# Splitting the first two input loads by head parity, and five idle matmuls in front of the last expert's rows, in a one-core attention and mixture kernel

## The chip, the cores and the metric

The kernel runs on one core of a Trainium2 chip. The core has five engines that work side by side: TensorE (PE, matrix products, with its weight loads listed apart as PEld), VectorE (DVE), ScalarE (ACT), GpSimd (POOL) and SyncE (SP), which here only issues transfers. Sixteen DMA engines move data between the chip's main memory and the core's memory. The metric is the device time of one execution in microseconds (us); lower is better.

## The reference

```python
def _attn_ref(r, k, v, w, u):                       # r, k, v: (4, 8, 768, 48), w, u: (8, 48)
    state = np.zeros((B, H, D, D))
    for t in range(S):
        kt, vt, rt = (k[:, :, t], v[:, :, t], r[:, :, t])
        cur = np.einsum('bhd,bhe->bhde', u[None] * kt, vt)
        y[:, :, t] = np.einsum('bhd,bhde->bhe', rt, state + cur)
        state = w[None, :, :, None] * state + np.einsum('bhd,bhe->bhde', kt, vt)

def _moe_ref(x, phi, w1, w2):                       # x: (3072, 384), phi: (384, 32), w1: (8, 384, 1024), w2: (8, 1024, 384)
    logits = x @ phi
    d = softmax(logits, axis=0)                     # over the tokens
    slot_input = (d.T @ x).reshape(E, 4, D)
    for e in range(E):
        slot_out[e] = np.maximum(slot_input[e] @ w1[e], 0.0) @ w2[e]
    c = softmax(logits, axis=1)                     # over the slots
    return c @ slot_out
```

A linear attention with a decaying state runs over four batches of 768 steps with eight heads of width 48. Its output, seen as 3072 tokens of width 384, goes through a soft mixture: each of eight experts has four slots, a slot is a weighted mean of all tokens, each expert runs two matrix products on its slots, and each token takes a weighted mean of the 32 results.

## The kernel before, in words

The kernel is a list of small named tasks. The string `ORDER` at the top (lines 9 to 31) gives the order in which they are emitted, and with it the order of the instructions on every engine; nothing is reordered later. An engine runs its own instructions strictly in that order and waits where one needs another engine's or a transfer's result.

**Front.** The inputs come in eight pieces m = 0 to 7, two for each batch: an even piece has 256 time steps of all eight heads, an odd one 512. Tasks `Lk`, `Lr` and `Lv` load k, r and v of a piece; all are issued by SP with `load_f` (line 192). In the tile, partition p holds eight (odd pieces: sixteen) consecutive steps of one head pair, first the even head, then the odd head. The source view puts the time blocks first, then the eight heads. A whole k or r of an even piece is one transfer of 256 runs of 1536 bytes, 384 KB. The decay vector w is loaded by ACT at line 211, and u by SP (task `LU`, line 381), between `Lr0` and `Lv0`.

`Sk0` and `Sr0` multiply the first k and r by tables of decay powers (line 427, on DVE for piece 0, mostly on POOL afterwards). The tables come from w: a logarithm on ACT (line 283), products on DVE (line 281), exponentials on ACT (line 287 and line 288). Then PE transposes the pieces (line 436), forms the attention scores (line 506) and the states, and writes the tokens' rows.

**Weights.** The 16 expert matrices are loaded by POOL with a conversion to bf16 (tasks `W0` to `W15`, lines 783 and 785) as buffers come free. The last one, the second matrix of the eighth expert, is in two transfers: `W15a` has seven of its eight row blocks and `W15` the last.

**Tail.** `Q00` to `Q13` (line 921) multiply the hidden values by the experts' second matrices and sum into one accumulator. `Q11` has the third expert of the second group, `Q12` the last expert's first seven row blocks (waits for `W15a`), and `Q13` its eighth (waits for `W15`). ACT copies the sum (`so`, line 928). Then 24 output rows of 128 tokens each are formed by PE (line 949), copied alternately by ACT and DVE (lines 951 and 953) and written by SP in eight transfers of 1, 2, 3, 4, 4, 4, 4 and 2 rows (line 955). Row 0 is made in two halves, one for each copying engine.

**Idle products.** A word such as `F19a_4` in `ORDER` stands for matmuls whose results nobody reads (line 861): the number after the underscore is the amount in units of 256 columns, issued as matmuls of up to 512 columns; the letter a says that they write the score accumulator `Ab`.

**Transfers and their semaphores.** The trace's instructions show that the transfers of SP and ACT take eight semaphores in turn, and that a transfer waits until the one eight places earlier has landed.

Of the kernel before, what the change touches and what calls it, by code (L numbers as in the profile page):

```python
# [26 lines left out]
NB1 L3 AL2 ET2 YE11 AC1 ZT2 RM3 EE2 ZC3 EX3 SU2 F10a_3 X111 X110 XE111:ACT AL3 F11a_1 ET3 W15a ND1 XE110 EE3:ACT LB4  # L27
RM4 DP2 G1 DP3 AC2 EX4 G2 ET4 AL4 G3 G5 LC2 GS EE4 F12_3 DP4 AC3 ZT3 AC4 LX1 NM2 NB2 F13a_1 MG UN SU3 LC3 F14_6 H00
R00:DVE NM3 H01 R01 F15a_5 HT00 ND2 W15 HT01 HE00 F16a_1 Q00 HE01 Q01 H11 LE1:ACT R11 H10 LX2 R10:DVE NB3 LT4 ND3:ACT
SU4 F18a_2 HT11 HT10 HE10 HE11:ACT LC4 NM4 NB4 ND4:DVE Q10 LE2 LX3 LX4 LE3 F19a_4 Q11 Q12 LE4:ACT Q13  # L30
"""


# [12 lines left out]
class _Plan:  # L46
# [7 lines left out]
    def buf(self, pool):  # L54
        return _Buf(pool)

    def add(self, name, engs, fn, deps=(), bufs=()):
        self.by[name] = _Task(name, engs, fn, list(deps), list(bufs))
# [23 lines left out]
def kernel(  # L82
# [13 lines left out]
    B, H, S, D = r.shape  # L96
# [11 lines left out]
    R = 8  # L108
# [5 lines left out]
    CC = NS // U3  # L114
# [11 lines left out]
    def O(ins):  # L126
        return tc.keep_in_program_order(ins)

    pe, dve, act, pool, sp = nc.tensor, nc.vector, nc.scalar, nc.gpsimd, nc.sync
# [5 lines left out]
    RW = 2 * J * D  # L135
# [53 lines left out]

    def load_f(dst, a, m):
        b, lg = divmod(m, 2)
        jn = J if lg else JH
        O(sp.dma_start(out=dst[:, 0:2 * jn * D].rearrange("p (e x) -> p e x", e=2),  # L195
                       in_=a[b].rearrange("h (y j) d -> y h (j d)", j=jn)[lg * CC * R:lg * CC * R + 32]))

# [146 lines left out]
    def consts_d():  # L344
# [5 lines left out]
    L = _Plan(dict(raw=raw, ks=ks_t, vj=vj_t, kn=kn_t, vn=vn_t, AT=AT_t, prs=pr_t[0:1], prl=pr_t[1:2], dv=dv_t,  # L350
                   **{f"{x}T": t for x, t in turned.items()},
                   S=S_t, Z=Z_t, x=x_t, zc=zc_t, Lc=Lc_t, Lcl=[Lc_t[0][:, NS - 2:]], Lsl=[Ls_t[0][:, NS - 2:]], Ls=Ls_t, E=E_t, ET=ET_t, T=T_t, A=[Ab], Y=[Yb], M=[Mb], **{f"xT{j}": [t] for j, t in enumerate(xT_t)}))
    buf, add = L.buf, L.add
# [17 lines left out]
    for m in range(NLD):  # L371
        for i, nm in enumerate("krv"):

            b, o = (kr["k", m][0], RH) if nm == "r" and m % 2 == 0 else (buf("raw"), 0)
            kr[nm, m] = b, o
            add(f"L{nm}{m}", "SP", (lambda b, o, a, m: lambda t: load_f(b.inst[:, o:RW], a, m))(b, o, (k, r, v)[i], m), bufs=[b])

    def load_phi(t):
        O(sp.dma_start(out=phi_f, in_=moe_phi.rearrange("(p q) s -> p q s", q=nM)))
# [13 lines left out]
    for h, av_, x in (("a", argl, slice(0, JH + 1)), ("b", argm, slice(JH, J + 1))):  # L393
        add(f"AH{h}", "DVE", (lambda av_, x: lambda t: argv_part(av_, e17l[:, x]))(av_, x))
        for i in range(2):

            add(f"TB{i}{h}", "ACT", (lambda i, h, av_: lambda t: O(act.activation(  # L397
                out=tabl[i][:, :, JH:J] if h == "b" else tabl[i][:, :, 0:JH],
                in_=av_[:, :, 1 - i:JH + 1 - i], func=AF.Exp, scale=(-1.0, 1.0)[i])))(i, h, av_),
# [3 lines left out]
    for m in range(NLD):  # L403
        lg = m % 2
        pb = TT["p", m] = buf("pr" + "sl"[lg])
        for nm in "krv":
            dstT = TT[nm, m] = buf(nm + "sl"[lg] + "T")
            P = P2 if nm == "v" else 128
            for h in range(1 + lg):
# [11 lines left out]
                else:  # L421
                    i = "kr".index(nm)
# [42 lines left out]
    for n in range(NU):  # L465
# [4 lines left out]
        m = 2 * bt + (ui > 0)  # L470
# [50 lines left out]
        def f_su(t, Mf=Mf, kn=kn, vn=vn, Sold=Sold, pb=pb, n=n, NK=NK):  # L521
# [13 lines left out]
            bufs=[Mf, vn, pb_, kn] + ([Sold] if ui else []))  # L535
# [26 lines left out]
        def f_y(t, Yf=Yf, rT=rT, vn=vn, dvb=dvb, Sold=Sold, Smid=Smid, a=tuple(ATb), n=n):  # L562
# [18 lines left out]
            bufs=[Yf, rTb, vn, dvb, Smid, ATb[0], ATb[1]] + ([Sold] if ui else []))  # L581
# [213 lines left out]
    for n in range(2 * E):  # L795
        wat[n] = buf("raw")
        wat[n].left += 4
        bufs, deps = [wat[n]], []
# [6 lines left out]
    nm = nm_t[(NPC - 1) % 2]  # L805
# [14 lines left out]
        bufs=[SXb])  # L820
# [118 lines left out]
    i = 0  # L939
# [46 lines left out]
```

## Time and profile before

| | us |
|---|---|
| median of three runs (118.89 to 119.31) | 119.17 |
| the profiled execution's own time | 120.24 |
| its span in the profile | 118.5 |
| PE busy | 98.0 (83%) |
| DVE busy | 94.8 (80%) |
| ACT busy | 86.6 (73%) |
| POOL busy | 61.0 (52%) |
| data moved by the DMA engines | 31.81 MB written to their targets, mean 268 GB/s |

The profile is of one execution, and times below are in microseconds from the start of its span. The span is 1.7 us shorter than that execution's own time, and the profiled execution took 1.1 us more than the median of the runs without a profile. A busy share is an average over stages that differ: what decides is what ended the last wait of each stage.

### The profile page before, as it was taken

To read this page: it belongs to the slowest core of one execution; us is meant where nothing else is said; L and a number is where in the kernel's file an instruction comes from. 1 tells how busy PE (TensorE), PEld (TensorE's weight loads), DVE (VectorE), ACT (ScalarE), POOL (GpSimd) and SP (SyncE) were. 2 spreads that over 40 slices of the span, in tenths; PEclk is the share of its full clock that TensorE was granted. 3 is DMA by queue.
4 is the path that set the end of the run, shared out by engine and by line. 5 is a ranking of instruction groups with operands and counts; after the bars stand their busy time and mean duration, and the time that the engine had idled before them with its cause. 6 is when DMAs were issued, how large, how long until landed. Compare 5 with 4: busy or idle time off the path is not lost.

```text
span 118.5 us, 3926 instructions
## 1 busy us (share of the span) xinstructions
PE 98.0 (83%) x1660; PEld 71.1 (60%) x1660; DVE 94.8 (80%) x180; ACT 86.6 (73%) x140; POOL 61.0 (52%) x79
## 2 busy tenths in 40 slices
PE   3997895999999999989999989999899985498000
PEld 0364674787888787867788878686453542254000
DVE  6899987898999999999999989999786274099100
ACT  5769894999999999989899799979644151269000
POOL 7605899999999989999999010002303000000000
PEclk9999999999999999999999999999999999869955
DMA  2999999999999999999999999999999995059994
GB/s 31 333 387 374 364 408 397 383 390 401 384 384 391 297 229 223 219 215 214 217 212 221 210 223 207 223 207 219 212 212 218 216 207 104 12 199 407 419 402 166
DMA packets 10441, 31.81 MB, mean 268 GB/s; under 512 B 1080, under 2 KB 4408, under 8 KB 10424
## 3 DMA queue, kind: packets, MB, share of 16 engines
q0 software_dynamic: 2448, 12.58, 51.8%
q1 hardware_dynamic: 7832, 18.93, 42.3%
q8 instruction: 13, 0.21, 0.7%
q10 hardware_dynamic: 144, 0.05, 0.2%
q14 instruction: 4, 0.03, 0.1%
HBM read 39.42 MB, written 4.72 MB: 373 GB/s over the span
## 4 chain that ended last, share of the span: by engine, by line
PE 32%; DMA 23%; POOL 15%; DVE 9%; ACT 6%; issue 4%; SPq 3%; DVEq 0%; ACTq 0%; POOLq 0%
DMA raw<-in_moe_w_dram 16%; POOL mix L427 12%; PE T L436 7%; DMA raw<-in_r_dram 7%; PE Ab L506 3%; DVE mix L953 2%; PE Yb L572 2%; SPq L195 2%; PE T L491 2%; PE Yb L567 2%; DVE AT_all L511 2%; ACT xT_all L359 2%; PE Yb L578 2%; PE T L481 2%; PE T L595 2%
## 5 line engine op out<-in xcount | busy, mean ns | idle before, releaser
L427 POOL TENSOR_TENSOR mix<-raw,tabl 128x768 bf16<-128x768 f32 x15 | 27.7, 1858 | 5.8 <-ACT tabl L397 5.4
L511 DVE TENSOR_TENSOR AT_all<-Ab,mask 128x1024 bf16<-128x1024 f32 x24 | 29.3, 1219 | 1.1 <-PE Ab L506 0.5
L359 ACT COPY mix<-T 128x1024 bf16<-128x1024 bf16 x19 | 19.1, 1021 | 3.9 <-PE T L436 2.3
L436 PEld LDWEIGHTS <-mix 128*128 128x128 bf16 x192 | 11.8, 99 | 2.3 <-DVE mix L427 0.7
L555 DVE TENSOR_TENSOR dv<-vn,Mb 128x768 bf16<-128x768 bf16 x12 | 11.4, 946 | 1.4 <-PE Mb L545 1.1
L427 POOL TENSOR_TENSOR mix<-raw,tabs 128x768 bf16<-128x768 f32 x6 | 10.8, 1815 | 0.0
L359 ACT COPY vT_all<-T 96x1024 bf16<-96x1024 bf16 x10 | 10.2, 1021 | 0.5 <-PE T L436 0.4
L506 PE MATMUL Ab<-mix 64*128 64x128 bf16 x192 | 9.5, 218 | 1.2 <-ACT mix L359 1.0
L359 ACT COPY xT_all<-T 128x768 bf16<-128x768 bf16 (+1 forms) x12 | 9.3, 784 | 1.3 <-PE T L595 1.3
L359 ACT CAST x<-Yb 128x768 bf16<-128x768 f32 x12 | 9.7, 808 | 0.0
L436 PE MATMUL T<-turnl,mix 128*128 128x128 bf16 x128 | 9.6, 219 | 0.1
L359 ACT COPY vn<-T 128x768 bf16<-128x768 bf16 x11 | 8.8, 814 | 0.0
L452 DVE TENSOR_TENSOR pr<-T,mix 128x1024 bf16<-128x1024 bf16 x12 | 8.0, 681 | 0.0
L712 POOL TENSOR_TENSOR Lc<-Ls,sm 128x192 bf16<-128x192 f32 x2 | 1.0, 516 | 13.5 <-ACT E L690 13.5
L506 PEld LDWEIGHTS <-mix 64*128 64x128 bf16 x192 | 5.8, 94 | 3.5 <-issue 0.7
L572 PEld LDWEIGHTS <-AT_all 128*128 128x128 bf16 x192 | 6.6, 96 | 1.6
L359 ACT COPY kn<-T 128x768 bf16<-128x768 bf16 (+1 forms) x10 | 7.2, 722 | 0.1
L418 POOL CAST vj<-raw 128x768 bf16<-128x768 f32 x8 | 6.7, 832 | 0.6 <-POOL phi_s L336 0.6
L436 PEld LDWEIGHTS <-vj 128*96 128x96 bf16 x96 | 6.2, 123 | 1.2 <-issue 0.2
L572 PE MATMUL Yb<-vn,AT_all 128*128 128x48 bf16 x192 | 6.8, 183 | 0.0
L539 DVE TENSOR_TENSOR Z<-Mb,wT 128x384 bf16<-128x384 f32 x12 | 6.6, 553 | 0.1
L481 PE MATMUL T<-ident,mix 128*128 128x128 bf16 x80 | 6.1, 219 | 0.2
(187 smaller groups left out, 237.8 us busy)
## 6 DMA issues: line engine op xcount, KB each, us to landing
raw<-in_moe_w_dram POOLq DMA_DIRECT2D x13, 768.0 KB, 14.4
raw<-in_k_dram SPq DMA_DIRECT2D x4, 768.0 KB, 12.2
raw<-in_r_dram SPq DMA_DIRECT2D x4, 768.0 KB, 12.2
raw<-in_v_dram SPq DMA_DIRECT2D x4, 768.0 KB, 12.2
out_dram<-mix SPq DMA_DIRECT2D x3, 768.0 KB, 4.6
raw<-in_k_dram SPq DMA_DIRECT2D x4, 384.0 KB, 10.9
raw<-in_r_dram SPq DMA_DIRECT2D x4, 384.0 KB, 10.6
raw<-in_v_dram SPq DMA_DIRECT2D x4, 384.0 KB, 10.8
```

The lines of the kernel that those rows point to most:

```text
L195: O(sp.dma_start(out=dst[:, 0:2 * jn * D].rearrange("p (e x) -> p e x", e=2), in_=a[b].rearrange("h (y j) d -> y h (j d)", j=jn)[lg * CC * ...
L359: O(act.copy(dst, src))
L418: O(act.copy(o, i_) if t.eng == "ACT" else pool.tensor_copy(o, i_))
L427: O(eng.tensor_mul(src.inst.rearrange("p (j e s) -> p e j s", j=JH, e=2)[:, :, :, 0:D], rv(), tab))
L436: O(pe.transpose(Tb.inst[0:P, jj * 128:(jj + 1) * 128], sv[:, jj, :], (turn, turnl)[lg][:]))
L452: O(dve.tensor_mul(cv(pb), tv(), cv(kT)))
L481: O(pe.transpose(Tb.inst[:, x * 128:(x + 1) * 128], kT.inst[:, x, :], ident[:]))
L506: O(pe.matmul(Abf.inst[:, e, x * C:(x + 1) * C], kT.inst[s, g * nQ + x, :], rT.inst[s, g * nQ + x, :]))
L511: O(dve.tensor_mul(AT.inst[:], Abf.inst[:].rearrange("p e (g t) -> p e g t", g=nQ), mask[:, None, None, :].to_broadcast([128, 2, nQ, C])))
L539: O(dve.tensor_mul(Smid.inst[:], Mf.inst[:, 0:SW].rearrange("p (q d) -> p q d", q=nQ)[:, :, None, :].to_broadcast([128, nQ, 2, D]), wT[:, ...
L555: O(dve.tensor_mul(dvb.inst[:].rearrange("p g e d -> p (g e) d"), vn.inst[:].rearrange("p g e d -> p (g e) d"), Mf.inst[:, 448:448 + 2 * P ...
L572: O(pe.matmul(y[:, x // nQ, q * P2 + e * D:q * P2 + (e + 1) * D], a[x // nQ].inst[:, e, q, :], vn.inst[:, x, e, :], start=False, stop=(c = ...
```

## The change

`load_f` gets a switch. With it, a load becomes two transfers: first the even heads of all time blocks, then the odd heads, each 128 runs of 1536 bytes (192 KB) into its half of every partition's row. The switch is set for the first k and the first r alone (piece 0). Every later load, and the first v, is unchanged. In `ORDER` one word is added, `F20a_10` between `Q11` and `Q12`: five idle matmuls of 512 columns into `Ab`.

```diff
-SU4 F18a_2 HT11 HT10 HE10 HE11:ACT LC4 NM4 NB4 ND4:DVE Q10 LE2 LX3 LX4 LE3 F19a_4 Q11 Q12 LE4:ACT Q13
+SU4 F18a_2 HT11 HT10 HE10 HE11:ACT LC4 NM4 NB4 ND4:DVE Q10 LE2 LX3 LX4 LE3 F19a_4 Q11 F20a_10 Q12 LE4:ACT Q13
...
-    def load_f(dst, a, m):
+    def load_f(dst, a, m, halves=False):
         b, lg = divmod(m, 2)
         jn = J if lg else JH
+        if halves:
+
+            for e in range(2):
+                O(sp.dma_start(out=dst[:, e * jn * D:(e + 1) * jn * D],
+                               in_=a[b].rearrange("(q e) (y j) d -> e y q (j d)", e=2, j=jn)[e, lg * CC * R:lg * CC * R + 32]))
+            return
         O(sp.dma_start(out=dst[:, 0:2 * jn * D].rearrange("p (e x) -> p e x", e=2),
...
-            add(f"L{nm}{m}", "SP", (lambda b, o, a, m: lambda t: load_f(b.inst[:, o:RW], a, m))(b, o, (k, r, v)[i], m), bufs=[b])
+            add(f"L{nm}{m}", "SP", (lambda b, o, a, m, hv: lambda t: load_f(b.inst[:, o:RW], a, m, hv))(b, o, (k, r, v)[i], m, m == 0 and i < 2), bufs=[b])
```

## The prediction

> **What bounds the kernel now.** I read the page's 40 slices first.
>
> ```profile
> PEclk9999999999999999999999999999999999869955
> DMA  2999999999999999999999999999999995059994
> GB/s 31 333 387 374 364 408 397 383 390 401 384 384 391 297 229 223 219 215 214 217 212 221 210 223 207 223 207 219 212 212 218 216 207 104 12 199 407 419 402 166
> ```
>
> The DMA row is the bound: full from the second slice (3 us) to the 33rd (98 us). The GB/s row halves from 40 us on because the weights arrive as half-size bf16; read as fp32 they are about 430 GB/s, the same pace. A stretch in which the DMA engines have nothing to do near the start is not made up later. After the hole at 100 us comes a second full stretch, the output.
>
> The chain of waits shows how the two stretches are joined:
>
> ```profile
> 82.73 18.82 DMA raw<-in_moe_w_dram
> 101.56 0.04 issue
> 101.60 0.51 PE Yb L921 x7
> 102.10 0.01 issue
> 102.11 0.34 PE Yb L921
> ```
>
> W15a is issued at 82.73 and lands at 101.56: 18.8 us for 672 KB, so it stands in a queue. Q12 runs as soon as it lands, Q13 after W15, then `so` at 102.47. So the end is the start of the transfer stream, its bytes, the 2.4 us from W15a to the first output product at 103.00, and the output.
>
> The windows: two of half a microsecond at the start, three of 1 us at the tail, and two of 3.41 us (columns: stretch, its length, busy time and instructions of PE, PEld, DVE, ACT, POOL, granted PE clock, DMA share, GB/s):
>
> ```profile
> 2.50:3.00 0.50, 0.00 (x0) 0.00 (x0) 0.50 (x4) 0.49 (x2) 0.50 (x5) 1.00 0.62 116
> 3.00:3.50 0.50, 0.34 (x3) 0.26 (x4) 0.50 (x4) 0.50 (x4) 0.50 (x4) 1.00 0.89 273
> ```
>
> ```profile
> 99.00:100.00 1.00, 0.42 (x8) 0.13 (x9) 0.00 (x1) 0.00 (x0) 0.00 (x0) 1.00 0.45 82
> 100.00:101.00 1.00, 0.00 (x0) 0.00 (x0) 0.00 (x0) 0.00 (x0) 0.00 (x0) 1.00 0.25 45
> ...
> 103.00:104.00 1.00, 1.00 (x5) 0.69 (x5) 0.45 (x2) 0.32 (x1) 0.00 (x0) 0.50 0.06 16
> ```
>
> ```profile
> 99.19:102.60 3.41, 1.06 (x16) 0.27 (x8) 0.00 (x0) 0.13 (x1) 0.00 (x0) 1.00 0.20 36
> ...
> 17.27:20.68 3.41, 2.13 (x36) 1.67 (x34) 2.43 (x4) 1.93 (x3) 3.41 (x3) 1.00 1.03 399
> ```
>
> The first two lines show the stream of loads starting and not yet full at 3 us. At the tail PE is idle from 99.42 to 101.60. Its granted clock falls to 0.50 at 102.60 and is back at 106.01, one stretch of 3.41 us. The first record of full clock is at 7.03, and 102.60 is 28 times 3.413 us later, so the clock seems to be judged on a grid of 3.41 us by what PE did in the stretch before: PE was busy 1.06 of 3.41 us (31%) ahead of the fall, and the least busy stretch that kept the full clock had 2.13 us (62%).
>
> Last, the timeline of SP's queue:
>
> ```profile
> 0.73 0.71 SPq L195 DMA_DIRECT2D raw<-in_k_dram  x1
> 1.49 0.80 SPq L195 DMA_DIRECT2D raw<-in_r_dram  x1
> 2.35 0.53 SPq L381 DMA_DIRECT2D LexpT<-in_u_dram  x1
> 2.91 0.60 SPq L195 DMA_DIRECT2D raw<-in_v_dram  x1
> ...
> 103.94 1.07 SPq L955 DMA_DIRECT2D out_dram<-vT_all  x2
> 105.83 3.61 SPq L955 DMA_DIRECT2D out_dram<-mix  x4
> ```
>
> By the packet records k's first packet starts at 2.42, 1.69 us after its issue began; r's follow at 4.0 and v's at 4.97 without a hole.
>
> **Part 1, the halves.** Removed: two issues, 0.71 + 0.80 with 0.05 behind each, 1.61 us. Added: four issues of 128 runs. Nearest rows: the first two output transfers, also from SP and also 128 pieces, take 0.35 each; w on ACT, 128 pieces from the same kind of source view, takes 0.63; u, four pieces, 0.53. So a half costs 0.35 to 0.63. I take 0.40: the output rows are the same queue and count, plus a little because k's first issue took 0.71 where v's, the same shape, took 0.60. Four are 4 x (0.40 + 0.05) = 1.80, so u, v0 and all behind them on SP are issued 0.19 later. v0 would start at 3.10, and its packets could flow by 3.10 + 1.69 = 4.79.
>
> The gain: a half has fewer runs to prepare, so its packets may start earlier. From end of issue to first packet k needed 0.98 and the first output 0.85 - 0.35 = 0.50 us (packets from 104.79). With the issue over at 1.13 that is 1.63 to 2.11 against 2.42, a gain of 0.31 to 0.79; w, with as many pieces, had its first packet at 2.16, a gain of 0.26; if the 1.69 runs from the start of the issue whatever the size, nothing. I take 0.31. Then k and r are through by 4.97 - 0.31 = 4.66, and v0's packets at 4.79 leave a hole of 0.13. Net 0.18, say **-0.20**, and since the DMA row never opens, it arrives at W15a whole. Ends: -0.79, and +0.74 (all four at 0.63: v0 issued 1.11 later, at 4.02, its packets at 5.71 against 4.97).
>
> Beside it: Sk0 and Sr0 wait for both halves, but start at 5.46 and about 6.3, when tables and DVE come free; k lands at 4.86 and r at 5.83, so there is 0.5 us of cover. w, which the tables wait for, lands at 3.41 and shares the DMA engines with k from 2.42 on; earlier packets of k could make it later by as much as they are earlier, 0.3 us. That moves the tables and the compute behind them, which has PE's 2.17 us wait for W15a as cover at the end. POOL at 12.48 waited 0.34 for r1 and follows the stream. On the semaphores every transfer from r3 on is still paired with the same earlier one; v1 to v2 now wait for k's and r's halves, landed before their issue (4.87 to 7.10). The later issues on POOL's queue are unmoved.
>
> **Part 2, the idle products.** Five matmuls of 512 columns. Two such rows at 98.39 and 98.60 stand 0.216 apart, so 1.08 us, from 99.42 to 100.50. W15a lands at 101.56, so 1.06 us of cover is left; if W15a came over 1.06 us earlier, the rest would be paid, at most 1.08. No other engine waits on them.
>
> What they bring: PE's busy share ahead of 102.60 becomes (1.06 + 1.08) / 3.41 = 63%, as in the least busy stretch that kept the clock. The price of the low clock, in this execution: output products are 0.32 apart instead of 0.16, and a half-row product takes 0.32 to 0.36 before its copy may start; at full clock the 384-column rows take 0.33 instead of 0.52, so for 192 columns I estimate 0.25. The second half row's product starts at 103.11 now and its copy on DVE at 103.52; at full clock that product would start at 103.08 and the copy 0.25 + 0.04 later, at 103.37, which is 0.15 earlier. DVE's chain to row 5 is one half row and three rows, 0.37 + 0.57 + 0.56 + 0.56 = 2.06, ending at 105.43 instead of 105.70. The third output transfer, issued at 105.83, waits for that copy, and from its first packet (106.67) to the end the DMA share is full. So **-0.27**.
>
> The grid can lie otherwise in other executions, which this trace can't show. A fall at 101.4 to 101.9 also slows Q12 and Q13 and costs some 0.3 more, -0.6 in all; one after 103.5 or none leaves 0. As the one execution shown, -0.27 is kept; ends 0 and -0.6. Above nothing: only if W15a comes early, as said.
>
> The Trainium skill (TensorE: Matmul & The Clock Gate, The HAM clock gate) has the clock fall only after an idle window of about 3.4 us, and its closing table asks for no PE gaps over about 3 us. By that rule the 2.17 us gap costs nothing, the idle products bring 0, and the sum is -0.20. The trace disagrees: the clock is 0.50 from 102.60 with no longer gap ahead of it.
>
> **Sum.** -0.20 - 0.27 = -0.47. The profiled execution's 120.24 would be 119.77. It stands 1.07 above the median of the runs, 119.17; with that difference taken as unchanged, the time is **118.70**.
>
> **Rivals.**
>
> *A. The halves bring nothing, the clock does.* The first packet depends on the start of the issue, or w's later landing takes it back: 119.17 - 0.27 = 118.90. For it: the first packets of all engines at 2.4 us are slow (0.6 to 0.7 us against 0.065 later), whatever the transfer. Against: w's at 2.16.
>
> *B. The clock is not held or had not fallen in most runs, the halves work:* 119.17 - 0.20 = 118.97. For it: 63% is only just the share that is known to hold. Against: 31% is far below. The Trainium skill's rule on the clock, above, would end here too.
>
> *C. The slower one: a half costs as much to issue as w, 0.63.* SP then feeds the DMA engines more slowly than they drain: a half is 192 KB, 0.49 us at 400 GB/s. v0's packets start at 5.71, the hole is 0.74, and 119.17 + 0.74 - 0.27 = 119.64. It outweighs the clock from 0.51 us a half on, and is a loss of over 0.3% from 0.60 on. For it: w's row, with the most similar view, and v's 0.60 for twice the runs. Against: the output rows' 0.35.
>
> *D. Each transfer has a cost on the DMA engines.* The first output took 0.68 us (104.79 to 105.47) for 192 KB, 0.20 above its share at 400 GB/s; two more transfers add 0.40: 119.17 + 0.40 - 0.27 = 119.30. Against: k's and r's packets follow each other closely. The Trainium skill (DMA: Bandwidth & Descriptors, Rules for kernel authors) asks for at least 1 MiB in a transfer, and these go from 384 to 192 KB; its fixed 2.0 us for each, not overlapped, would make an estimated +4.0 and 122.9. The packets without a hole between k and r speak against that.
>
> *E. More than forecast:* output-like latency, -0.79, with the dearer fall, -0.6: 117.78.
>
> **How the numbers follow.** No change means within 0.3% of 119.17, 0.36 us, about what a measurement of this kernel can tell. Forecast 0.45 and E 0.05 are faster: 0.50. A 0.14, B 0.12 and D 0.04 are no change: 0.30. C 0.17 and the odd mishap beside it, 0.03, are slower: 0.20. The predicted time is the forecast's 118.70, its own range 118.2 to 118.8. The range goes from 118.2 to 119.6: E, half of C and the mishap lie outside.
>
> **What would show it.** First packets before 2.2 and four SP issues of about 0.4; v0's packets without a hole; W15a landing 0.2 earlier; a granted clock of 1.00 from 99 to 107; output products 0.16 apart; the third output issue about 0.5 earlier. It is wrong if the halves' issues are near 0.6, if a hole stands in the DMA row near 5 us, or if the clock still falls.

## The result and the profile after

Before 119.53 us (median of 22 runs, 118.86 to 121.16), after 120.28 us (median of 22 runs, 119.66 to 121.35). The ratio is 1.0063, with an interval of 1.0040 to 1.0087: the change makes the kernel slower by 0.6%, 0.75 us. Forecast were 118.70 and a range of 118.2 to 119.6.

The one profiled execution of after took 119.75 us, less than the 120.24 of the profiled execution of before. Single executions of the same code lie up to 2.3 us apart here, so a profile is read for its starts and durations, and the verdict comes from the many runs.

Three rows of the 40 slices of after:

```profile
PEclk9999999999999999999999999999999999999965
DMA  2899999999999999999999999999999998149994
GB/s 54 249 344 396 391 392 397 387 385 397 390 382 388 335 236 224 215 218 215 215 214 215 216 213 214 217 214 221 210 215 219 213 213 158 25 177 421 402 421 179
```

The second slice (3 to 6 us) has an 8 in the DMA row where before has a 9, and 249 and 344 GB/s stand where before has 333 and 387. At the tail the clock row stays at 9. SP's queue at the start of after (start, duration, instructions of that line):

```profile
0.73 1.27 SPq L198 DMA_DIRECT2D raw<-in_k_dram  x2
2.05 1.24 SPq L198 DMA_DIRECT2D raw<-in_r_dram  x2
3.33 0.52 SPq L387 DMA_DIRECT2D LexpT<-in_u_dram  x1
3.90 0.62 SPq L201 DMA_DIRECT2D raw<-in_v_dram  x1
```

Two halves take 1.27 and 1.24 us with the short step between them; one by one they take 0.58 to 0.63, as much as the whole v0 (0.62), which has twice the runs. v0 is issued at 3.90 instead of 2.91, 0.99 later. The stretches of 1 us that follow, before and then after (columns as in the prediction, the DMA share and the GB/s last):

```profile
4.00:5.00 1.00, 1.00 (x4) 0.32 (x3) 0.98 (x3) 0.61 (x2) 0.95 (x4) 1.00 1.05 376
5.00:6.00 1.00, 1.00 (x3) 0.29 (x2) 0.89 (x3) 1.00 (x2) 0.00 (x0) 1.00 0.98 301
6.00:7.00 1.00, 1.00 (x8) 0.53 (x7) 1.00 (x2) 0.31 (x2) 0.00 (x0) 1.00 1.05 407
```

```profile
2.50:3.00 0.50, 0.00 (x0) 0.00 (x0) 0.50 (x5) 0.49 (x2) 0.50 (x5) 1.00 0.79 280
...
4.00:5.00 1.00, 1.00 (x4) 0.34 (x3) 0.85 (x2) 0.33 (x2) 0.94 (x4) 1.00 0.83 234
5.00:6.00 1.00, 1.00 (x3) 0.29 (x2) 0.85 (x5) 1.00 (x3) 0.00 (x0) 1.00 0.78 174
6.00:7.00 1.00, 0.78 (x4) 0.13 (x3) 1.00 (x2) 0.72 (x2) 0.00 (x0) 1.00 0.76 253
```

The stream starts earlier (280 GB/s in 2.50:3.00 against 116), then falls: from 4 to 7 us before moved 1084 KB and after 661 KB. The packet records show the whole of it. I added up the bytes of the load packets in the order in which they end and compared the times at which the same amount was through: after is 0.36 us ahead at 0.2 MB, 0.85 behind at 1.0 MB, and 0.54 behind at 10 MB. From there to the end of the weights the lag stays (0.61 at 25 MB), since the DMA row has no gap in which to catch up. How much two executions of the same code differ, a second profile of the kernel before shows (c_before): 0.37 behind at 1.0 MB, but 0.21 ahead at 4 MB and 0.03 ahead at 10 MB. So the value at 10 MB is the one to trust.

At the tail, the last part of the chain of waits in after:

```profile
83.41 17.91 DMA raw<-in_moe_w_dram
101.32 0.04 issue
101.36 0.84 PE Yb L927 x8
102.22 0.49 ACT so L934
```

W15a lands at 101.32, in this profile even before the 101.56 of before. A landing is that of the slowest of 16 DMA engines. In before the median engine was through with W15a at 99.24 and the slowest 2.32 later; in after the median was at 99.70 (0.46 later, the hole) and the slowest only 1.62 later. That last distance was between 1.5 and 2.9 us in all profiles, in no order that goes with the edits.

The stretch of the clock's grid that corresponds to the one ahead of the fall in before (28 times 3.413 us behind the first record of full clock, which is at 6.98 here), in after:

```profile
99.14:102.55 3.41, 2.96 (x25) 0.90 (x23) 0.54 (x2) 0.70 (x2) 0.00 (x0) 1.00 0.29 52
```

PE is busy for 2.96 of 3.41 us and the clock stays at 1.00 until 112.79. Output products stand 0.16 apart, and the third output transfer is issued at 105.02 instead of 105.83. So the second part did at the clock what it was to do.

### The profile page after: what moved, and what is told of

Same layout as the page of the kernel before. It is cut to its first block, busy times and chain, and to the rows that moved or that the text cites. A ratio compares the mean times of both kernels' runs of the same rounds, so it can differ in the third digit from the quotient of the medians.

```text
span 118.0 us, 3934 instructions
## 1 busy us (share of the span) xinstructions
PE 98.4 (83%) x1661; PEld 71.1 (60%) x1665; DVE 94.1 (80%) x180; ACT 87.0 (74%) x140; POOL 61.4 (52%) x79
## 4 chain that ended last, share of the span: by engine, by line
PE 39%; DMA 18%; ACT 14%; DVE 13%; issue 4%; POOL 4%; DVEq 0%; ACTq 0%; POOLq 0%
DMA raw<-in_moe_w_dram 15%; PE T L442 9%; PE Ab L512 4%; DVE mix L959 3%; PE Yb L578 3%; POOL mix L433 3%; DMA LexpT<-in_w_dram 3%; ACT tabl L403 3%; PE Yb L573 3%; ACT mix L365 2%; PE Yb L584 2%; PE T L487 2%; PE Mb L535 2%; PE Mb L538 2%; PE T L601 2%
## 5 line engine op out<-in xcount | busy, mean ns | idle before, releaser
L867 PE MATMUL Ab<-mix,ident 128*128 128x512 bf16 (+1 forms) x25 | 6.4, 346 | 0.1
```

What stands on the lines that cost most here:

```text
L867: O(pe.matmul(o[:, 0:256 * min(n, 2)], ident[:], mix[:, 0:256 * min(n, 2)], start=True, stop=True))
```

## The experiments

The theory after the result, called S: each half costs SP a full issue, v0 and all behind it are issued 1 us later, the stream has a hole near 5 us and never makes it up. Rivals: P, the idle products stand in front of Q12 and cost; T, w lands later (3.81 instead of 3.41), and the tables and the compute behind them are late; D, a split load costs by itself (the expectations call it H). A fifth, that v0's own readers are held up, is answered by the trace: ACT's first conversion of v0 starts at 8.48 in after, 8.29 in before, and in neither does ACT stand idle ahead of it. Every kernel had 12 timed runs (e14 10) against 21 to 35 of before on the same chip. Shifts of the stream are those at 10 MB in the one profile of each, against the profile of before.

| run | edit | stream, us | ratio to before (interval) |
|---|---|---|---|
| e1_fill | idle products alone | -0.18 | 0.9989 (0.9960 to 1.0019) |
| e1b_fill | the same again | -0.31 | 0.9994 (0.9963 to 1.0026) |
| e12_fill_double | ten instead of five | 0.00 | 1.0043 (1.0009 to 1.0076) |
| e2_halves | halves alone | +0.84 | 1.0063 (1.0023 to 1.0103) |
| e2b_halves | the same again | +0.79 | 1.0092 (1.0061 to 1.0122) |
| e3_two_tiny | two tiny loads ahead of v0 | +0.15 | 0.9994 (0.9965 to 1.0023) |
| e8_four_tiny | four tiny loads ahead of v0 | +0.61 | 1.0004 (0.9972 to 1.0037) |
| e8b_four_tiny | the same again | +0.61 | 1.0072 (1.0037 to 1.0107) |
| e10_halves_v0_act | halves, v0 issued by ACT | +0.15 | 0.9993 (0.9953 to 1.0033) |
| e11_k_two_queues | k's halves on SP and ACT | -0.66 | 1.0005 (0.9971 to 1.0040) |
| e4_halves_u_late | halves, u behind k1 | +1.14 | 1.0062 (1.0021 to 1.0103) |
| e5_khalf_u_late | k in halves, u behind k1 | +0.51 | 1.0002 (0.9964 to 1.0041) |
| e9_u_late | u behind k1 alone | +0.37 | 1.0027 (0.9987 to 1.0068) |
| e6_w_late | tiny load ahead of w on ACT | -0.53 | 0.9973 (0.9941 to 1.0005) |
| e6b_w_late | the same again | -0.39 | 0.9949 (0.9917 to 0.9980) |
| e13_u_on_act | u on ACT ahead of w | +0.02 | 1.0003 (0.9961 to 1.0046) |
| e14_after_u_on_act | after, u on ACT ahead of w | +0.91 | 1.0088 (1.0055 to 1.0121) |
| c_before | before, unchanged | -0.03 | 0.9982 (0.9944 to 1.0021) |

### One part at a time: e1_fill, e2_halves, e2b_halves

```diff
-... F19a_4 Q11 Q12 LE4:ACT Q13
+... F19a_4 Q11 F20a_10 Q12 LE4:ACT Q13
```

> The five idle products alone, loads as before. Theory S (the stream of transfers sets the end; the halves opened a hole in it, the idle products work): 0 to 0.3 us faster than before, and the granted clock does not fall between 99 and 107. Rival P (the idle products are what costs, by running into W15a's landing or by what they do to PE): about the 0.75 us slower that the whole change was.

The halves alone are the change without that word.

> The halves alone, no idle products. Theory S: slower by 0.75 to 1.0 us, at least as slow as the whole change; four SP issues of about 0.62, the same bytes moved 0.85 us later at 1 MB and about 0.55 later from 6 MB on. Rival P: no difference to before.

> The halves alone again, beside the four tiny loads on the same chip. Theory S (the hole in the stream of transfers at 5 us): 0.75 us slower. Rival H (the halved transfers themselves, not the hole): the same 0.75.

The idle products alone change nothing that can be told (0.9989), the halves alone cost 1.0063 and, once more, 1.0092. So P falls, and the halves carry the whole loss. Three stretches of e2_halves show the hole of after:

```profile
4.00:5.00 1.00, 1.00 (x4) 0.35 (x3) 0.79 (x2) 0.33 (x2) 0.94 (x4) 1.00 0.83 246
5.00:6.00 1.00, 1.00 (x3) 0.30 (x2) 0.85 (x5) 1.00 (x3) 0.00 (x0) 1.00 0.75 172
6.00:7.00 1.00, 0.72 (x3) 0.06 (x2) 1.00 (x2) 0.78 (x2) 0.00 (x0) 1.00 0.77 233
```

### The hole without the halves: e3_two_tiny, e8_four_tiny, e8b_four_tiny

k and r stay whole. Extra loads of u's four pieces into unused tiles stand on SP between u and v0; nobody reads them. e3 has two, e8 and e8b four.

```diff
+    spare = [cst.tile([nQ, P2], f32, name=f"spare{j}") for j in range(4)]
+    for j in range(4):
+        add(f"LZ{j}", "SP", (lambda j: lambda t: O(sp.dma_start(out=spare[j][:], in_=u.rearrange("(q e) d -> q (e d)", e=2))))(j))
...
-CB0 Lk0 Sk0 Lr0 Tk0 Sr0 LU Lv0 ...
+CB0 Lk0 Sk0 Lr0 Tk0 Sr0 LU LZ0 LZ1 LZ2 LZ3 Lv0 ...
```

> First k and r whole as before, but two more tiny loads (1.5 KB each, into spare tiles that nobody reads) on SP between u and the first v. It delays v0's issue by some 1.16 us without halving anything and without touching w. Theory S: v0 is issued near 4.07, its packets start near 5.76 instead of 4.97, and the time is 0.6 to 0.8 us longer. Rival T (what costs is that w lands later beside k's earlier packets, so that the tables and the compute behind them start late): w lands at 3.41 as before, no difference to before.

> The stronger dose of the two tiny loads, which were cheaper to issue (0.30 each) than thought: four of them between u and the first v, k and r whole. v0 should be issued near 4.1 (with the halves it was 3.9) and its packets start near 5.8. Theory S (a hole in the stream at 5 us is paid at the end): 0.6 to 0.9 us slower. Rival H (it is not the hole but the halved transfers themselves, slower packets or the consumers' second wait): no difference to before.

> The four tiny loads again, beside the halves. Theory S: as slow as the halves within 0.3 us, 0.4 to 0.9 us slower than before, since its hole is as large (0.85 us at 1.2 MB). Rival H: within 0.2 us of before, as it was the first time.

Two were too small a dose, and the expectation missed: the tiny loads took only 0.27 and 0.30 us, v0 was issued at 3.56 and the stream lost 0.15. Four give the delay of the change, and a hole, as SP's queue and the stretches of e8b_four_tiny show:

```profile
2.92 1.28 SPq L384 DMA_DIRECT2D spare<-in_u_dram  x4
4.24 0.61 SPq L195 DMA_DIRECT2D raw<-in_v_dram  x1
```

```profile
4.00:5.00 1.00, 1.00 (x4) 0.32 (x3) 1.00 (x3) 0.57 (x2) 0.94 (x4) 1.00 1.06 387
5.00:6.00 1.00, 1.00 (x3) 0.29 (x2) 0.85 (x3) 1.00 (x2) 0.00 (x0) 1.00 0.39 94
```

The first comparison gave 1.0004, as rival H said and not S; the second gave 1.0072, as S said. Together that is about +0.4%. The stream's lag was 0.61 in both profiles, and the kernel itself took about as long both times (120.16 and 120.30); it was the kernel before that took 120.13 on the first chip and 119.46 on the second. Why is not known. So a hole without halves probably costs, but these runs do not show it surely; the size of the cost is taken from e2 and e2b.

### The halves without the hole: e10_halves_v0_act, e11_k_two_queues

```diff
+    O(act.dma_start(out=raw[1][:, 0:2 * JH * D].rearrange("p (e x) -> p e x", e=2),
+                    in_=v[0].rearrange("h (y j) d -> y h (j d)", j=JH)[0:32]))
     O(act.preload_act_table_set("natural_log_exp_and_others"))
...
-    def load_f(dst, a, m):
+    def load_f(dst, a, m, halves=False):
+        if a is v and m == 0:
+            return
```

k and r are in halves as in after, without the idle products; v0 is issued by ACT right behind w, so it does not wait for SP.

> Both halves as in the change, no idle products, but the first v is issued by ACT right behind w, near 1.4, so that the stream has v0's packets to move while SP is still issuing the halves. Theory S: no hole, the stream 0.2 to 0.4 us earlier than before and the time 0 to 0.4 us shorter than before. Rival H: still about 0.75 us slower.

ACT's queue at the start, and the stretches:

```profile
0.73 0.65 ACTq L219 DMA_DIRECT2D LexpT<-in_w_dram  x1
1.40 0.87 ACTq L220 DMA_DIRECT2D raw<-in_v_dram  x1
```

```profile
4.00:5.00 1.00, 0.93 (x4) 0.51 (x5) 0.36 (x1) 0.61 (x4) 0.94 (x4) 1.00 0.74 230
5.00:6.00 1.00, 1.00 (x3) 0.29 (x2) 0.96 (x4) 0.72 (x2) 0.00 (x0) 1.00 1.00 338
6.00:7.00 1.00, 1.00 (x4) 0.29 (x2) 0.89 (x3) 1.00 (x3) 0.00 (x0) 1.00 1.00 351
```

Same split, but the DMA share is back at 1.00 from 5 us on, the lag is 0.15, and the ratio is 0.9993 where e2b_halves, in the same comparison, has 1.0092. So D falls as far as these runs go: the split costs nothing that can be told once v0 does not wait for SP. No run has v0 on ACT with k and r whole, so a gain from the shorter queue of SP could hide a small cost; but e13, where v0 is issued 0.76 earlier by SP and nothing is split, gained nothing (1.0003).

The Trainium skill (Trainium Kernel Development and Optimization, Key Constraints) says that issuing from several engines at once saves only the issue time of the sequencer. This trace fits: v0's issue takes 0.87 us on ACT, beside the halves on SP, and SP issues k1 at 3.89 instead of 4.57 in after.

In e11 the first k's even half is issued by SP, its odd half by ACT ahead of w, at the same time; r is whole.

```diff
+    O(act.dma_start(out=raw[0][:, JH * D:2 * JH * D],
+                    in_=k[0].rearrange("(q e) (y j) d -> e y q (j d)", e=2, j=JH)[1, 0:32]))
     O(act.dma_start(out=w_f, in_=w.rearrange(...
```

> The first k in two halves, the even heads on SP and the odd heads on ACT ahead of w; the first r whole. SP then has 0.1 us less to issue than before in front of v0, and the first packet should start near 2.14 instead of 2.42. If the issue time on SP is what the halves cost, there is no hole near 5 us, the stream is 0.2 to 0.4 ahead and the ratio is 0.997 to 1.000. If a split of a load costs by itself, wherever it is issued, the ratio is 1.003 (half of what the two splits cost). w is issued 0.6 later, which cost nothing in the run with w late.

The stream was ahead, -0.66 at 10 MB, as S asks, but in that profile it lost this between 14 and 15 MB (39 to 44 us), where the last input loads end (+0.10 at 25 MB), and the ratio is 1.0005. The ratio gives no sign of a loss by the split, but its interval (to 1.0040) still holds the 1.003 that rival D asked for.

### A later w: e6_w_late, e6b_w_late

```diff
+    spare = cst.tile([nQ, P2], f32, name="spare")
+    O(act.dma_start(out=spare[:], in_=u.rearrange("(q e) d -> q (e d)", e=2)))
     O(act.dma_start(out=w_f, in_=w.rearrange(...
```

> Loads on SP as before, but ACT issues a tiny load (1.5 KB into a spare tile) ahead of w, so that w and ACT's first work come some 0.6 us later. Theory S: the transfers are where they were and PE has 2.2 us of cover at the end, so the difference is under 0.2 us. Rival T: w landing 0.4 us later was the cost, so 0.6 us later costs 0.6 to 0.9 us.

> The run with a tiny load ahead of w on ACT, once more. If a later w costs nothing but brings nothing either: 0.998 to 1.002. If the first time's 0.9973 was a gain (its stream of transfers was 0.5 us ahead in the one profile): 0.996 to 0.999. A cost of w's later landing that would explain the changed kernel asks for 1.004 or more.

The logarithm starts at 4.74 (4.70 in e6b) instead of 3.43 and `Sk0` at 6.7 instead of 5.46, three times the delay that the halves brought, and neither run is slower: T falls. Both are even faster, 0.9973 and 0.9949. That was not expected.

### Moving u: e4_halves_u_late, e5_khalf_u_late, e9_u_late, e13_u_on_act, e14_after_u_on_act

In e4, e5 and e9 u's load goes behind k1 on SP, to give back 0.55 us to v0; e4 splits k and r, e5 only k, e9 nothing.

```diff
-CB0 Lk0 Sk0 Lr0 Tk0 Sr0 LU Lv0 Ek0:ACT VC0:ACT Lk1 AHa ...
+CB0 Lk0 Sk0 Lr0 Tk0 Sr0 Lv0 Ek0:ACT VC0:ACT Lk1 LU AHa ...
```

> Both halves as in the change, no idle products, but u is issued behind the first v and the second k, so that v0 is issued 0.58 earlier, near 3.33. Theory S: the shift of the stream shrinks from about 0.85 to about 0.3 us, so 0.1 to 0.4 us slower than before instead of 0.75. Rival H: as slow as the halves alone, 0.75.

> Only k in halves, r whole, u behind the first v and the second k: v0 is issued near 2.9 as before, and the first packet comes 0.28 earlier. Theory S: no hole, the stream 0.2 to 0.3 us earlier, 0.1 to 0.3 us faster than before. Rival H: half of the halves' cost, 0.3 to 0.4 us slower.

> The loads as before, u behind the first v and the second k: the yardstick for the two kernels that move u. v0's issue comes 0.58 earlier, but the stream had no hole there. Theory S: within 0.15 us of before. Rival H says the same.

None of the three came out clearly as S expected: e4 was as slow as rival H said (0.75 us), e5 was neither faster nor slower, and e9, which was to change nothing, has 1.0027, with 1 inside its interval. At 1.0 MB the three lag less than after does (+0.32, +0.05, +0.39 against +0.85; the unchanged c_before has +0.37 there), but each then loses 0.35 to 0.8 us more up to 2 or 4 MB (only e9 makes a part of it up), where single issues of SP take 0.9 to 1.3 us. Why is not settled. e9, with no split, is at +0.37 already, so e4 and e5 do not tell the halves from the move. e4's time (1.0062) still goes with its stream (+1.14).

e13 and e14 take u off SP and issue it on ACT ahead of w; e13 is before, e14 after.

```diff
+    O(act.dma_start(out=u_f[0:nQ], in_=u.rearrange("(q e) d -> q (e d)", e=2)))
     O(act.dma_start(out=w_f, in_=w.rearrange(...
...
-    add("LU", "SP", lambda t: O(sp.dma_start(out=u_f[0:nQ], in_=u.rearrange("(q e) d -> q (e d)", e=2))))
+    add("LU", "SP", lambda t: None)
```

> The kernel before with u's load taken off SP and issued by ACT ahead of w. SP issues v0 0.55 us earlier, at about 2.35, and w starts 0.6 later. If the gain of the two runs with w late (0.9973 and 0.9949) comes from the later compute, which then meets W15a with a shorter gap on PE and a full clock, it is here again: 0.994 to 0.998. If it came from the extra load itself or was chance: 0.998 to 1.002.

> The changed kernel (halves and idle products) with u's load on ACT ahead of w. v0 is issued at about 3.35 instead of 3.90, so half of the hole near 5 us is closed: +0.4 of the changed kernel's +0.9 against the kernel before, less 0.3 for the earlier first packet, nearly nothing. But the later compute (1.2 us) and the idle products (1.08 us) now take the same gap in front of W15a, which is 0 to 2.2 us wide: the idle products then stand on the path by about 1 us in most executions, 1.003 to 1.009. If the gap is usually 2 us or more, they stay hidden: 0.995 to 1.000.

e13 has w as late as e6 (logarithm at 5.18) and no gain: 1.0003, stream +0.02. So the lateness of w is not what made e6 faster. What did stays open: e6 and e6b had the stream 0.53 and 0.39 us ahead, about their gain, but no run shows why.

e14 was to close half of the hole. It did not: r's two halves took 1.45 us, v0 was issued at 3.55, and the stream lagged by 0.91. Its 1.0088 lies in the expected range for another reason than the one expected: in its profile the idle products begin at 100.48 and take 1.25, and W15a lands at 102.65, 0.9 us later, so the loss is the hole's.

### The idle products' cover: e1b_fill, e12_fill_double

```diff
-... F19a_4 Q11 F20a_10 Q12 LE4:ACT Q13
+... F19a_4 Q11 F20a_20 Q12 LE4:ACT Q13
```

e1b repeats e1, e12 doubles the products (the `-` line is e1).

> The five idle products alone, once more. The forecast of -0.27 us asks for 0.998; the theory that they gain in some executions and stand in front of Q12 in others asks for 0.998 to 1.001. A cost that alone would explain the slower time of the changed kernel asks for 1.004 or more.

> Idle products alone, ten instead of five: 10 x 0.216 = 2.16 us between Q11 and Q12. In the profiles of executions without them, PE waited from 0 to 2.2 us in front of W15a. If that cover is about 1 us on average, ten products run past W15a's landing by 1.1 us on average, and what they save at the clock is at most 0.3: ratio 1.004 to 1.010. If the cover is nearly always 2.2 as in the profile of the kernel before, the ten cost nothing and hold the clock at least as well as five: 0.997 to 1.000.

Five are free to 0.3% twice; ten cost 0.43%, 0.5 us. So the cover ends between 1.1 and 2.2 us in a typical execution. In the profile of e1b_fill five were already on the chain that ended last:

```profile
100.13 1.19 PE Ab L861 x5
101.31 0.64 PE Yb L921 x8
```

W15a had landed at 101.06, so Q12 started 0.25 late.

### The unchanged kernel: c_before

> The kernel before once more, as a yardstick: a ratio of 1.000 within its interval, and a second trace of the same code, to see how much the landing of the last expert's weights differs from one execution to the next. Both theories say the same.

It came out at 0.9982, so differences of 0.2% between two such sets of runs mean nothing here. Its stream is 0.03 ahead at 10 MB; those of e1, e1b and e12, whose loads are untouched too, are 0 to 0.31 ahead, so a shift of 0.3 us can be chance.

Read down, the table says the same as the single tests. Eight profiles, after's with its +0.54 included, show the stream over 0.5 us late; but for e5 and the first e8 these are the ones 0.6% or more slower. Of those at +0.15 or less only the doubled products are slower.

## Why the prediction was wrong, point by point

**The bound: right.** The stream sets the end in before and after; a hole at 5 us was still there at 10 and 25 MB (+0.54, +0.61). It has little room over the compute: in e6, e6b, e10 and e11, where ACT's first work starts 0.6 to 0.9 us later, PE goes from Q11 to Q12 without a wait for W15a, so there the compute is as late as the stream.

**The issue of a half: wrong, and this step failed.** "So a half costs 0.35 to 0.63. I take 0.40: the output rows are the same queue and count". It measured 0.58 to 0.63, and 0.64 to 0.68 with the step to the next issue, so the four took 2.60 us in place of 1.80. The row to take was the nearest in kind, a load with the same kind of source view (w's 0.63, and v's 0.60 for twice the runs). That v and w cost the same with 256 and 128 runs stood in the profile and spoke against a price by the number of runs. The text named this as rival C and gave it 0.17.

**The first packet: right in the number, partly by luck.** Forecast 0.31 earlier; it starts at 2.14 instead of 2.42, 0.28 earlier, and after is 0.36 ahead at 0.2 MB. But the working had the issue over at 1.13 and the packet 0.98 behind it; the issue was over at 1.36 and the packet came 0.78 behind it, and the two misses cancel. It is worth nothing if v0 comes too late behind it.

**The hole: 0.13 forecast, 0.74 in rival C.** v0's issue came 0.99 later, and the lag at 1.0 MB was 0.85. The term of -0.20 measured +0.54 in after's stream and, by the times of e2 and e2b (1.0063 and 1.0092 of 119.5), +0.75 to +1.1.

**Beside it: right.** w landed 0.40 later (3.41 to 3.81), where 0.3 was allowed for, and a later w cost nothing (e6).

**The clock: mechanism right, size wrong.** With the products the clock held in the profiles of after, e1, e1b, e12 and e14. The term of -0.27 came from one execution. Own time minus W15a's landing tells what a fall costs: 18.58 to 18.72 in before, e2, e5 and e9, where the clock fell between 102.6 and 103.2; 18.03 to 18.52 in e4, e8 and e8b, where it fell at 103.7 or later; 18.04 to 18.43 in the seven without products where it held (e2b, e3, e6, e6b, e10, e11, e13). So an early fall costs about 0.4 (means 18.64 and 18.24), but it was in 4 of the 9 profiles in which PE stood idle for over a microsecond. That makes 0.18 on average. (A tenth, c_before's, fell too, at 102.43, with 18.83.) Against it, kernels with products have a mean of 18.35, 0.11 above those where the clock held alone. By this estimate 0.07 is left, which no comparison here can show: e1 and e1b measured 0.13 and 0.07 less, both within 0.3%.

**The cover: too wide.** "1.06 us of cover is left" was read from one execution, and the five products held up Q12's place in the queue for 1.19 us (e1b), where 1.08 was forecast. Q11 starts between 98.9 and 99.6 and W15a lands between 101.01 and 102.17 in the kernels without halves and with u and w in their places (before, e1, e1b, e3, e8, e8b, e12), and the two vary on their own.

The result is 1.58 us above the forecast of 118.70. Of this, 0.36 is the base: the kernel before has a median of 119.53 in 22 runs and had 119.17 in the three that the forecast started from. The rest is the sum of the two terms: 0.75 to 1.1 in place of -0.20, and about -0.1 in place of -0.27.

## What to carry to other kernels

Where a queue's issues follow each other closely and the data behind them are the bound, count instructions on that queue, not bytes: two loads in place of one cost an issue more (about 0.6 us here; 0.5 for each split, since the whole k and r had taken 0.71 and 0.80), and everything behind them starts later. Price an added instruction by the row that is like it in kind, direction and source view, and look whether rows of different sizes cost the same. A gain read from a wait of one execution, such as a clock that falls after it, has to be weighed by how often that wait comes.

## What was not expected of the hardware

- Most loads' issues on SP take the same for 128 runs (0.58 to 0.64) as for 256 (0.60 to 0.62), an output's 128 pieces 0.35, and a tiny load's four pieces 0.26 to 0.66, least when the same load was issued just before.
- Between 102 and 106 us the clock fell after stretches of its grid in which PE was busy for 31% (before) to 50% (e9), and it held after stretches with 51% (e2b) and 59% (e3). The lines of e9 and e2b:

```profile
99.75:103.17 3.42, 1.72 (x19) 0.48 (x17) 0.48 (x2) 0.70 (x2) 0.00 (x0) 1.00 0.17 31
98.94:102.35 3.41, 1.73 (x25) 0.67 (x17) 1.24 (x5) 0.37 (x1) 0.00 (x0) 1.00 0.42 79
```

The length of the gap does not tell the two cases apart: PE stood idle for 1.32 us in e9 and for 1.87 in e2b. The busy share is no full rule either, since in the output stage the clock fell behind stretches with 55% and 56% (e6b, e10, at 109.1). The Trainium skill (TensorE: Matmul & The Clock Gate, The HAM clock gate) speaks of an idle window of that length; here the clock fell behind windows that were up to 50% busy.
- The last of 16 DMA engines was 1.5 to 2.9 us behind the median one with W15a, whatever the edit. The records also have 13 instruction fetches of 16 KB, 0.9 to 1.4 us each in before and after; whether they make this lag was not tried.
- A useless tiny load on ACT ahead of w came with a faster kernel twice (0.9973, 0.9949), and a useful load in its place did not (1.0003). It is the only version here with an interval wholly below 1 (e6b), and its cause is open.
